# The end of a three-stage kernel: the last slot sums added on TensorE, the combine weights turned by VectorE, the output multiplied transposed in fp32 row tiles, and freed buffers handed to the experts' loads

## The chip, the cores and the metric

One core of one Trainium2 chip runs the kernel. The metric is the device time of one execution in microseconds (us); for the kernel before it is the median of three runs.

## What is computed

Three stages follow each other. A local and a pooled attention give 2304 tokens of 512 features; a gated product turns each token x into (x w_a) * (x w_b) w_out; a soft mixture of experts closes. Only the last stage is touched by the change:

```python
logits = x @ phi                      # 2304 tokens x 32 slots
d = softmax of logits over the tokens
slot_input = d.T @ x                  # 32 slots x 512, eight experts of four slots
h = np.maximum(slot_input[e] @ w1[e], 0.0)
slot_out[e] = h @ w2[e]               # w1, w2: 8 x 512 x 1024 and 8 x 1024 x 512, fp32
c = softmax of logits over the slots
return (c @ slot_out).astype(np.float32)
```

## The kernel before

The tokens are cut into six groups of 384 (`GS`, `NG = 6`). For every group twelve units of 128 hidden features run on TensorE (`plan_unit`: `half(0)`, `half(1)`, L1076), VectorE multiplies the two halves (`gmul`, L1091) into the group's buffer `g`, and after four units `logits` (L1099) multiplies them by `wpr`, the router folded with w_out, 32 columns at a time into four column groups of one PSUM bank.

`plan_chain(c)` is the softmax of a group. ScalarE copies the logits (`k1`), a matmul with `rep` adds the four column groups (`k2`, L1145), VectorE takes the maximum (`k3`, L1151, L1153), ScalarE forms the correction factor `al` and the exponentials (`k4`, L1159, L1163), VectorE turns the exponentials (`k6`, L1181) and the features (`turn`, L1107), TensorE sums the tokens of each slot in 32x32 tiles (`k11`, L1222, four PSUM banks), and VectorE adds them to the running sum `acc` (`k12`, L1235: acc = acc * al + new). The same chain makes the combine weights `cn` (`kl` to `k10`).

After the last group comes `plan_tail`. `atr` (L1325) multiplies `acc` by `rep32`, which adds its four parts and turns them; `slot_in` (L1351) applies w_out; `si_tr` (L1363) turns the slots; `l1` (L1392) runs the first expert layer, `htr` (L1408) turns its result, `l2` (L1480) runs the second layer in three pieces of 256, 128 and 128 output columns (`PARTS`). For each piece `so_sum` (L1500) gathers the slots' outputs, `so_hi` and `so_lo` (L1505, L1509) split them in two fp32r parts, `om` (L1527) multiplies by the combine weights, `oe` copies PSUM to SBUF (L321 on ScalarE, L323 on VectorE) and `od` (L1540) stores. The combine weights are turned by `ctr` (L1448, 18 transposes of 128x128 on TensorE) and split by L1451 and L1458 into `cT`. Where the planner expects TensorE to wait, `fill` (L370) issues matmuls that nobody reads.

The experts' weights come in 64 loads of 512 KB (L1297), in the order in which they are used; the first 32 are w1, the others w2. All loads and stores stand in one queue (SP). A load waits for a buffer of the list `e4`; buffers join it when the work that held them is done: weights of the gated product, `x` of the last group, `g` of the last two groups, the tiles `ot` of w_out after `slot_in`, and each expert buffer after its use.

A planner (`Plan.run`) puts all tasks in an order at build time by durations written beside them; on the chip the order on each engine is fixed, and the waits are semaphores.

Of the kernel before, what the change touches and what calls it, by code (L numbers as in the profile page):

```python
# [108 lines left out]
def tokens_of(o):  # L109

    o, parts = o.reshape(-1), []
    for c0, w in PARTS:
        t = o[c0 * NTILES * 128:(c0 + w) * NTILES * 128].reshape(128, NTILES, w)
        parts.append(t.transpose(1, 0, 2).reshape(NTILES * 128, w))
    return np.concatenate(parts, 1)
# [166 lines left out]
def tile_attn_glu_softmoe(  # L282
# [323 lines left out]
    def plan_datt(b):  # L606
        pr = PR_D[b] + 1

        def dvload2(j):
            if j == 0:  # L610
# [21 lines left out]
        def dvmm(f):  # L632

            if f:
                X.pop("vdt")
# [358 lines left out]
    def plan_rows():  # L994

        for n in range(12):
# [10 lines left out]
            def stage(n=n, fc=fc, m=m):  # L1007
                r0 = fc * 512 + m * 128
                nc.sync.dma_start(out=X["ost"][n % 2], in_=w_out[r0:r0 + 128, :])

            def low(e, n=n):
                clow(X["ost"][n % 2], e)

            def ab(n=n):
                X["op", n] = psum()
                cabs(X["ost"][n % 2], X["op", n])

            def bits(n=n):
                cbits(X["ost"][n % 2], X["op", n])

            def sign(n=n, fc=fc, m=m):
                csign(X["ost"][n % 2], X.pop(("op", n)), X["o", fc, m])
# [14 lines left out]
    def plan_wprime(fc):  # L1037
# [12 lines left out]
        def e3():  # L1050
            nc.scalar.copy(out=wpr[:, fc * 4:fc * 4 + 4, :], in_=X.pop(("wq", fc)))
# [4 lines left out]
        T["wpr", fc] = add("A", 0.3, e3, [t], -5, rel=("ps",))  # L1056
# [11 lines left out]
    def plan_unit(g, k, n):  # L1068
        fc, fi = divmod(k, 4)
        gt = GS[g]  # L1070

# [23 lines left out]
        def logits():  # L1095
            if fc == 0:
                X["lg", g] = psum((128, gt))
            for y in range(4):
                nc.tensor.matmul(  # L1099
                    out=X["lg", g][y * 32:y * 32 + 32, :], lhsT=wpr[:, fc * 4 + y, :], rhs=X["g", g][:, fc * 4 + y, :],  # L1100
                    start=(fc == 0), stop=(fc == 2),
                )

        def turn(y):

            t = X["g", g][:, fc * 4 + y:fc * 4 + y + 2, :].rearrange("p a b -> p (a b)")
# [14 lines left out]
        if fi == 3:  # L1121
            t = add(
                "PE", gt * 0.00167 + 0.1, logits, [T["gt", g, fc * 4 + y] for y in range(4)] + [T.get(("lgl", g))] + [T["wpr", f] for f in range(3)],
# [3 lines left out]
            for y in (0, 2):  # L1127
                T.setdefault(("g", g), []).append(add("V", gt / 480 + 0.17, lambda y=y: turn(y), [t], -15 + 0.1 * fc))

# [5 lines left out]
    def plan_chain(c):  # L1135
        gt = GS[c]
        nt, t0 = gt // 128, G0[c] // 128

# [4 lines left out]
        def k2():  # L1143
            X["lt", c] = ps = psum((128, gt))
            nc.tensor.matmul(  # L1145
                out=ps, lhsT=rep, rhs=X["lgs", c], start=True, stop=True
# [8 lines left out]

        def k4():
            if c > 0:
                X["al", c] = sb(mp, "al", (128, 1))
                nc.scalar.activation(  # L1159
                    out=X["al", c], in_=X.pop(("nm", c - 1)), func=ACTF.Exp, bias=X["nm", c], scale=-1.0  # L1160
                )
# [65 lines left out]
        def k12():  # L1227
# [11 lines left out]
        t2 = add("PE", gt * 0.00167 + 0.02, k2, [t1], p - 1000, acq=("ps",))  # L1239
        t3 = add("V", gt / 960 + 0.2, k3, [t2, T.get(("k3", c - 1))], -28, acq=("nm",))  # L1240
        T["k3", c] = t3
        t4 = add(
            "A", 0.9 if c else 0.6, k4, [t3], -28, acq=(("al",) if c else ()) + ("sm",), rel=("nm",) if c else (),
        )
        t5 = add("V", 0.15, k5, [t4, T.get(("k5", c - 1))], -20, acq=("L",), rel=("sm",) + (("L",) if c else ()))
        T["k5", c] = t5
        t6 = add("V", gt / 960 + 0.17, k6, [t4], -28, acq=())
        tl = add("V", 0.9, kl, [t3], -27, acq=("lc",))
# [6 lines left out]
        held = [add("N", 0.0, lambda: None, [t3], 0, acq=("ps",), lat=0.0) for _ in range(4)]  # L1255
        t11 = add("PE", gt * 0.007 + 0.1, k11, [t6] + T["g", c] + held, p - 1000, rel=("lgs", "g"), part="32x32")
        t12 = add(
            "V", 2.4, k12, [t11, t5, T.get(("k12", c - 1))], -18, rel=("ps",) * 4 + (("al",) if c else ())
        )
        T["k12", c], T["k2", c], T["k11", c] = t12, t2, t11  # L1260


    def plan_tail():
# [13 lines left out]
        g = NG - 1  # L1277
        give(T["mm", g], (), 3, lambda: (X.pop(("xh", g)), X.pop(("xl", g)), X.pop(("xt", g)), cut(sb(mp, "x", (128, 8 * GT)), 3))[3])
# [43 lines left out]
        def atr():  # L1322
            X["aps"] = ps = psum((128, 12, 32))
            for k in range(12):
                nc.tensor.matmul(out=ps[:, k, :], lhsT=acc[:, k].rearrange("p q j -> p (q j)"), rhs=rep32, start=True, stop=True)  # L1325

        def aev():
            t = sb(X["tp"], "tl", (128, 512))
# [10 lines left out]
        ta = [add("A", 0.5, aev, [t], -50, rel=("ps",))]  # L1339
# [46 lines left out]
        for eg in range(2):  # L1386
            for hf in range(2):
# [30 lines left out]
                for dt in range(4):  # L1418
                    w = tw[0, eg, hf, dt]
                    t = add(  # L1420
                        "PE", 0.94, lambda dt=dt, l1=l1: l1(dt), [t_si[dt // 2], t] + w, 3000 + eg * 2 + hf,
# [3 lines left out]
                t = add("PE", 0.5, htr, [t] + hs[-1:], -1000, acq=("ps",), rel=("ht",))  # L1425
# [3 lines left out]
        def ct():  # L1429
            X.pop(("xh", NG - 2)), X.pop(("xl", NG - 2)), X.pop(("xt", NG - 2))  # L1430
            t = sb(mp, "x", (128, NTILES, 128), F32R)
            for x in range(0, NTILES, 2):
                X["cT", x] = t[:, x:x + 2, :]

        t_ct = add("N", 0.0, ct, T["mm", NG - 2], 0, lat=0.0)
        tc_ = []
        n = 2
        for i0 in range(0, NTILES, n):

            def crep(e, i0=i0, n=n):  # L1440
                X["c4", i0] = t = sb(X["tp"], "ht", (128, n, 4, 32))
                copy(e, t, view(cn, [[32, n], [0, 4], [1, 32]], i0 * 32))

            def ctr(i0=i0, n=n):
                X["ctp", i0] = ps = psum((128, n, 128))
                t = X.pop(("c4", i0))
                for i in range(n):
                    nc.tensor.transpose(out=ps[:, i, :], in_=t[:, i, :, :], identity=ident)  # L1448

            def chi(i0=i0, n=n):  # L1450
                nc.scalar.copy(out=X["cT", i0], in_=X["ctp", i0])  # L1451

            def clo(i0=i0, n=n):
                ps = X.pop(("ctp", i0))
                cT = X["cT", i0]
                for r0 in (32, 96):
                    r = slice(r0, r0 + 32)
                    nc.vector.tensor_tensor(  # L1458
                        out=cT[r], in0=ps[r], in1=cT[r].bitcast(F32), op=ALU.subtract
                    )  # L1460

            t = add("V", 0.4, crep, [t_ct, T["open"]] + [T["cn", c] for c in sorted({GROUP[i0], GROUP[i0 + n - 1]})],
                    50, acq=("ht",), alt=("G", 0.5))
            t = add("PE", 0.12 * n, ctr, [t],
                    3000 + i0 * 0.01 - 10, acq=("ps", "ctp"), rel=("ht",))
            t = add("A", 0.2 * n, chi, [t], 50)

            tc_.append(add("V", 0.86, clo, [t, T["k12", NG - 1] if i0 < 8 else t_si[1]], 50, rel=("ps", "ctp")))

        for dh, (col0, w) in enumerate(PARTS):  # L1470
# [15 lines left out]
            for eg in range(2):  # L1486
                for m in range(8 // nf):
                    tl = tw[1, dh, eg, m]
                    prev = add(
                        "PE", 1.02, lambda eg=eg, m=m, l2=l2: l2(eg, m), [hs[eg * 2 + (m * nf + nf - 1) // 4], prev] + tl,  # L1490
# [11 lines left out]
            def so_hi(dh=dh, cols=cols):  # L1502
                if dh == 0:
                    X["s4"] = sb(X["tp"], "ht", (128, 512), F32R)
                nc.scalar.copy(out=X["s4"][:, cols], in_=X["sop", dh])  # L1505

            def so_lo(dh=dh, cols=cols):
                lo = X["s4"][64:128, cols]
                nc.vector.tensor_tensor(out=lo, in0=X.pop(("sop", dh))[64:128], in1=lo.bitcast(F32), op=ALU.subtract)  # L1509

            t = add("A", 0.15 + 0.22 * w / 256, so_ev, [prev], -40, acq=("a",), rel=("ps",))
            t = add("PE", 0.43 * w / 256, so_sum, [t], -1000, acq=("ps",), rel=("a",))
            t = add("A", 0.15 + 0.22 * w / 256, so_hi, [t, T.get("s4")], -40, acq=() if dh else ("ht",))
            T.setdefault("s4", t)
            t = add("V", 0.38, so_lo, [t], -40, rel=("ps",))
            pend = []

            ng = -(-NTILES // nf)
            for c in range(ng):
                i0, n = c * nf, min(nf, NTILES - c * nf)  # L1520

                def om(c=c, i0=i0, n=n, cols=cols, dh=dh, w=w):
                    if c % 2 == 0:
                        X["ob", dh, c // 2] = X["e4"].pop(0)
                    X["om", dh, c] = psum((128, n, w))
                    for x in range(n):
                        nc.tensor.matmul(  # L1527
                            out=X["om", dh, c][:, x, :], lhsT=X["cT", (i0 + x) // 2 * 2][:, (i0 + x) % 2, :],
# [120 lines left out]
```

## Time and profile before

| | |
|---|---|
| median of three runs | 518.35 us (517.28 to 519.37) |
| span of the profiled execution | 515.9 us |
| runs' median less that span | 2.45 us |
| TensorE matmuls busy | 493.5 us, 96% of the span |
| VectorE, ScalarE, GpSimd busy | 282.1, 194.7, 129.1 us |
| share of the chain that ended last on TensorE | 67% |
| HBM read, written | 78.81 MB, 4.72 MB |

The profiled execution shows no time of its own beside its span; the three runs were timed apart from it, so the difference of 2.45 us holds what lies around the span and the scatter between executions. Busy time of TensorE counts the filling matmuls too, so it doesn't say what work remains; the chain of work that ended last does, stretch by stretch. Times in the rows are counted from the start of the span.

### The profile page before, as it was taken

How to read it: one execution, taken by the hardware profiler on the slowest of the kernel's cores; microseconds unless marked ns; L12 is line 12 of the kernel's file. 1: busy time of each engine (PE TensorE's matmuls, PEld its weight loads, DVE VectorE, ACT ScalarE, POOL GpSimd, SP SyncE). 2: the span in 40 equal slices, each digit the busy share in tenths (PEclk: the TensorE clock that was granted, in tenths of full speed). 3: DMA queues.
4: the chain of work that ended last, by engine and by line, in shares of the span. 5: the costliest groups of instructions: out<-in, count | busy, mean ns of one | idle time of the engine just before them, and what ended most of it. 6: DMA issues, size and time to landing. Idle time of an engine off the chain costs nothing.

```text
span 515.9 us, 12483 instructions
## 1 busy us (share of the span) xinstructions
PE 493.5 (96%) x5182; PEld 427.6 (83%) x5182; DVE 282.1 (55%) x621; ACT 194.7 (38%) x469; POOL 129.1 (25%) x192
## 2 busy tenths in 40 slices
PE   8899999998999999999998999999999999999995
PEld 7788878977888788998887998879999997984474
DVE  5798888449934477213876322572553616365022
ACT  0986878645444232211342222232434212112132
POOL 1499886518720100100446000120000000000000
PEclk9999999999999999999999999999999999999998
DMA  8948772256752000000442000202678555998998
GB/s 314 352 134 252 259 236 90 83 164 204 234 194 82 1 1 3 1 1 22 157 160 52 1 1 0 62 4 84 209 279 271 170 180 166 336 338 289 410 408 335
DMA packets 30265, 84.35 MB, mean 163 GB/s; under 512 B 3456, under 2 KB 4480, under 8 KB 30208
## 3 DMA queue, kind: packets, MB, share of 16 engines
q1 hardware_dynamic: 30208, 83.54, 46.9%
q8 instruction: 41, 0.67, 0.5%
q14 instruction: 16, 0.13, 0.1%
HBM read 78.81 MB, written 4.72 MB: 162 GB/s over the span
## 4 chain that ended last, share of the span: by engine, by line
PE 67%; POOL 10%; DVE 9%; DMA 7%; ACT 3%; issue 3%; POOLq 0%; DVEq 0%; ACTq 0%
PE ps L1076 43%; DMA qk<-in_qk_dram 3%; PE ps L1480 3%; PE ps L1392 3%; POOL e L326 3%; PE ps L1099 3%; POOL w L326 3%; PE ps L1222 2%; POOL dT L448 2%; PE ps L366 2%; DMA bv<-in_vd_dram 2%; PE ps L542 1%; PE ps L1527 1%; DMA w<-in_moe_w_a_dram 1%; DMA sw<-in_w_outt_dram 1%
## 5 line engine op out<-in xcount | busy, mean ns | idle before, releaser
L1076 PE MATMUL ps<-x,w 128*128 128x384 f32 x1728 | 319.1, 339 | 0.9 <-DVE x L326 0.9
L1076 PEld LDWEIGHTS ps<-x,w 128*128 128x128 f32 x1728 | 297.5, 188 | 14.7 <-issue 8.9
L1091 DVE TENSOR_TENSOR g<-a,ps 128x384 f32<-128x384 f32 x72 | 39.5, 549 | 81.6 <-PE ps L1076 76.9
L321 ACT COPY a<-ps 128x384 f32<-128x384 f32 x72 | 34.5, 479 | 123.3 <-PE ps L1076 116.7
L1107 DVE STREAM_TRANSPOSE g<-g 128x768 f32<-128x768 f32 x36 | 32.6, 951 | 10.1 <-PE ps L1099 10.0
L1209 POOL TENSOR_TENSOR cn<-lc,cs 128x96 f32<-128x96 f32 x6 | 2.1, 349 | 118.9 <-DVE cs L1206 118.9
L326 POOL TENSOR_TENSOR w<-w,w 128x512 fp32r<-128x512 f32 x20 | 26.7, 1341 | 7.4 <-ACT w L321 7.2
L366 PE MATMUL ps<-acc 128*128 128x128 f32 x152 | 22.2, 301 | 2.2 <-POOL acc L361 2.2
L326 POOL TENSOR_TENSOR e<-e,mx 128x512 f32<-128x512 f32 x20 | 21.3, 1067 | 6.7 <-DVE mx L518 6.7
L366 PEld LDWEIGHTS ps<-acc 128*128 128x128 f32 x152 | 20.3, 212 | 2.8 <-POOL acc L361 2.2
L887 DVE SCALAR_TENSOR_TENSOR ps<-ps,w8x 128x512 uint32<-128x512 uint32 x12 | 8.4, 699 | 22.4 <-ACT ps L883 22.3
L551 DVE TENSOR_TENSOR xn<-ps,xd 128x232 f32<-128x232 f32 (+1 forms) x40 | 13.8, 388 | 12.3 <-PE ps L542 11.6
L446 POOL TENSOR_TENSOR dT<-qk 128x116 f32<-128x116 f32 (+1 forms) x18 | 8.8, 489 | 41.1 <-DMA qk<-in_qk_dram 41.1
L887 DVE SCALAR_TENSOR_TENSOR ps<-ps,sw 128x512 uint32<-128x512 uint32 x16 | 11.1, 695 | 14.0 <-ACT ps L883 14.0
L448 POOL TENSOR_TENSOR dT<-dT,qk 128x116 f32<-128x116 f32 (+1 forms) x36 | 18.0, 499 | 2.8
L528 PE MATMUL ps<-cst,e 128*128 128x128 f32 x80 | 12.7, 281 | 6.2 <-POOL e L326 6.2
L878 ACT ACTIVATE w8x<-w8x 128x512 uint32<-128x512 uint32 x12 | 8.1, 672 | 27.1 <-DMA w8x<-in_moe_w_out_dram 27.1
L326 POOL TENSOR_TENSOR x<-xn,x 128x464 fp32r<-128x464 f32 (+5 forms) x10 | 8.7, 877 | 38.1 <-ACT x L321 38.1
L542 PEld LDWEIGHTS ps<-e,bv 64*64 64x64 f32 x640 | 12.4, 133 | 6.8 <-ACT e L321 3.0
L326 POOL TENSOR_TENSOR dk<-de,dm 128x128 f32<-128x128 f32 x9 | 3.6, 402 | 55.7 <-DVE dm L708 55.5
L878 ACT ACTIVATE w<-w 128x512 uint32<-128x512 uint32 x20 | 13.5, 681 | 9.7 <-DMA w<-in_moe_w_a_dram 6.0
L321 ACT CAST x<-xn 128x464 fp32r<-128x464 f32 (+5 forms) x24 | 12.0, 511 | 13.5 <-DVE xn L551 13.5
(163 smaller groups left out, 674.1 us busy)
## 6 DMA issues: line engine op xcount, KB each, us to landing
w<-in_moe_w_dram SPq DMA_DIRECT2D x39, 512.0 KB, 8.5
qk<-in_qk_dram SPq DMA_DIRECT2D x17, 480.0 KB, 5.0
w8x<-in_moe_w_dram SPq DMA_DIRECT2D x14, 512.0 KB, 7.9
sw<-in_w_outt_dram SPq DMA_DIRECT2D x12, 512.0 KB, 4.3
w8x<-in_moe_w_out_dram SPq DMA_DIRECT2D x12, 512.0 KB, 4.8
w<-in_moe_w_a_dram SPq DMA_DIRECT2D x10, 512.0 KB, 5.0
bv<-in_vw_dram SPq DMA_DIRECT2D x20, 256.0 KB, 3.5
w<-in_moe_w_b_dram SPq DMA_DIRECT2D x10, 512.0 KB, 4.3
```

The source lines that it names most:

```text
L321: nc.scalar.copy(out=out, in_=in_)
L326: (nc.vector if e == "V" else nc.gpsimd).tensor_tensor(**a)
L366: nc.tensor.matmul(out=X["warm"][:, 0:128], lhsT=acc[:, 0], rhs=acc[:, 0], start=True, stop=True)
L448: nc.gpsimd.tensor_tensor(out=dst, in0=dst, in1=one[r], op=ALU.add)
L542: nc.tensor.matmul(out=pss[hl][o:o + 64, hq // 2, bi * w:bi * w + w], lhsT=v[r, bi, hq, :], rhs=pt[r, hq, bi * 64:bi * 64 + w], start=True ...
L878: nc.scalar.activation(out=d, in_=d, func=ACTF.Copy, scale=31 / 32 * 2.0 ** -29, bias=-0.26)
L887: nc.vector.scalar_tensor_tensor(out=d, in0=d, scalar=3, in1=words(raw)[1], op0=ALU.logical_shift_left, op1=ALU.bitwise_or)
L1076: nc.tensor.matmul(out=ps, lhsT=X["w", fc, ab, fi // 2, wi][:, fi % 2, hq, :], rhs=X[x, g][:, hq, :], start=(hq == 0 and m == 0), stop=(hq ...
L1091: nc.vector.tensor_tensor(out=X["g", g][:, k, :], in0=X.pop(("a", g, k)), in1=X.pop(("mm", g, k, 1)), op=ALU.mult)
L1099: nc.tensor.matmul(out=X["lg", g][y * 32:y * 32 + 32, :], lhsT=wpr[:, fc * 4 + y, :], rhs=X["g", g][:, fc * 4 + y, :], start=(fc == 0), st ...
L1107: nc.vector.transpose(out=t, in_=t)
L1392: nc.tensor.matmul(out=X["l1", eg, hf][e * 32:e * 32 + 32, :], lhsT=X["siT"][:, dt, :], rhs=X.pop((0, eg, hf, dt, e)), start=(dt == 0), st ...
```

## The change

Eight edits, all of them at the end of the program but for one small copy and one load that is issued earlier.

1. In the last group the logits of units 8 to 10 are multiplied before the last half unit; those of unit 11 are added straight into the bank of the summed logits by one more matmul (`kd`) whose weights are `phis`, unit 11's router columns written four times side by side (one ScalarE copy in `plan_wprime`).
2. `k4` is split; the factor `al` is a task of its own. In the last group the exponentials come ahead of the turning of the logits (`kl`).
3. The last group has no `k12`. `plan_sum` instead scales `rep32` by `al` (`scaled`), adds the old `acc` into a fresh PSUM bank (`old`, four matmuls of 32 columns), copies the four new sums into `acc` (`out`, two on ScalarE and two on VectorE) and adds them into the same bank (`new`, four matmuls).
4. `atr` is gone: VectorE turns that bank into `aT`.
5. The combine weights are turned in place by one VectorE instruction of 128x576 (`turned`); the copies, transposes and splits of `cT` are gone.
6. `so_hi`, `so_lo` become one fp32 copy. `om` now has the slots' outputs as weights and the combine weights as moving operand: four matmuls of 32 rows x 128 columns x 288 tokens, each in its own row group and PSUM bank; eight such sets instead of three times 18 matmuls. `oe` copies 32 pieces of 288 columns.
7. The output lies transposed in memory: twelve stores of 864, 864 and 576 columns; the host puts it in order again.
8. `e4` gets five buffers more: three of the fifth group's `x` (before: `cT`), one more `w8x`, and two thirds of `acc` after `new`.

```diff
             for y in range(4):
+                if last and fc * 4 + y == 11:
+                    break
                 nc.tensor.matmul(
                     out=X["lg", g][y * 32:y * 32 + 32, :], lhsT=wpr[:, fc * 4 + y, :], rhs=X["g", g][:, fc * 4 + y, :],
...
+        def kd():
+            nc.tensor.matmul(
+                out=X["lt", c], lhsT=phis.rearrange("p a b -> p (a b)"), rhs=X["g", c][:, 11, :], start=False, stop=True
             )
...
+    def plan_sum():
...
+        def scaled():
+            X["alr"] = phis[:, 0, :]
+            nc.vector.tensor_scalar_mul(out=X["alr"], in0=rep32, scalar1=X["al", c])
+
+        def old():
+            X["sum"] = ps = psum((128, 384))
+            t = X.pop("alr")
+            for q in range(4):
+                nc.tensor.matmul(out=ps[q * 32:q * 32 + 32, :], lhsT=t, rhs=acc[:, :, q, :], start=True, stop=False)
+
+        def out(q, e):
+            copy(e, acc[:, :, q, :], X["da", c][q].rearrange("p (k j) -> p k j", k=12))
+
+        def new(q):
+            nc.tensor.matmul(out=X["sum"][q * 32:q * 32 + 32, :], lhsT=rep32, rhs=acc[:, :, q, :], start=False, stop=True)
...
+        for g in (NG - 2, NG - 1):
+            give(T["mm", g], (), 3, lambda g=g: (
+                X.pop(("xh", g)), X.pop(("xl", g)), X.pop(("xt", g)), cut(sb(mp, "x", (128, 8 * GT)), 3))[3])
...
-            nc.scalar.copy(out=X["aT"], in_=X.pop("aps"))
-
-        t = add("PE", 1.35, atr, [T["k12", c9]], -2000, acq=("ps", "tl", "lgs", "a"))
+            nc.vector.transpose(out=X["aT"].rearrange("p a b -> p (a b)"), in_=X.pop("sum"))
...
+        def turned():
+            t = cn.rearrange("p m s -> p (m s)")
+            nc.vector.transpose(out=t, in_=t)
...
+                    def om(hh=hh, d0=d0):
+                        for q in range(4):
+                            r = slice(32 * q, 32 * q + 32)
+                            X["om", d0, hh * 4 + q] = ps = psum((128, 288))
+                            nc.tensor.matmul(
+                                out=ps, lhsT=X["s4"][r, d0:d0 + 128], rhs=cn[r, 9 * hh:9 * hh + 9, :].rearrange("p m s -> p (m s)"),
+                                start=True, stop=True,
+                            )
```

TensorE, from the end of the gated product to `slot_in`. Before (matmuls that write 32 rows use 32 columns of the array; `cst` holds `ident`, `rep` and `rep32`):

```order
L370 MATMUL ps<-cst 128x128 x3
L1099 MATMUL ps<-g,wpr 32x384 x4
L370 MATMUL ps<-cst 128x128 x4
L1145 MATMUL ps<-lgs,cst 128x384
L370 MATMUL ps<-cst 128x128 x14
L1222 MATMUL ps<-g,lgs 32x384 x48
L370 MATMUL ps<-cst 128x128 x12
L1325 MATMUL ps<-cst,acc 128x32 x12
L1448 MATMUL ps<-cst,ht 128x128 x4
L370 MATMUL ps<-cst 128x128
L1351 MATMUL ps<-w8x,a 32x256 x12
```

The same place in the changed kernel, from behind the last half unit (three logits matmuls, L1104, stand ahead of that half):

```order
L1156 MATMUL ps<-lgs,cst 128x384
L1161 MATMUL ps<-g,phis 128x384
L367 MATMUL ps<-cst 128x128 x8
L1298 MATMUL ps<-acc,phis 32x384 x4
L367 MATMUL ps<-cst 128x128
L1239 MATMUL ps<-g,lgs 32x384 x48
L367 MATMUL ps<-cst 128x128 x4
L1304 MATMUL ps<-acc,cst 32x384 x4
L367 MATMUL ps<-cst 128x128 x4
L1402 MATMUL ps<-w8x,a 32x256 x24
```

The logits matmul between the last unit and the sum is replaced by `kd` (L1161); the old sum (L1298) stands ahead of `k11` (L1239), the new one (L1304) behind it in the place of `atr`; both halves of `slot_in` (L1402) follow each other without a transpose between them.

TensorE, the last rows of the program. Before:

```order
L1480 MATMUL ps<-w_5009,tl 32x128 x8
L1480 MATMUL ps<-w_5037,tl 32x128 x8
L1500 MATMUL ps<-a,cst 128x128
L1527 MATMUL ps<-ht,x 128x128 x18
```

In the changed kernel:

```order
L1496 MATMUL ps<-w8x,acc 32x128 x8
L1535 MATMUL ps<-cn,ht 128x288 x4
L1496 MATMUL ps<-w8x,acc 32x128 x8
L1496 MATMUL ps<-w_4887,acc 32x128 x8
L1516 MATMUL ps<-a,cst 128x128
L1535 MATMUL ps<-cn,ht 128x288 x8
```

The product with the combine weights (L1535) comes in sets of four between the loads' matmuls of `l2` (L1496), six sets ahead of the last `so_sum` (L1516) and two behind it.

SP's queue around the end of the fifth group's units. Before:

```order
L1297 DMA w_5009<-in_moe_w_dram 128x1024
L1297 DMA w_5036<-in_moe_w_dram 128x1024
L1297 DMA w_5037<-in_moe_w_dram 128x1024
L1297 DMA w_5172<-in_moe_w_dram 128x1024
```

In the changed kernel:

```order
L1349 DMA w_5012<-in_moe_w_dram 128x1024
L1349 DMA x<-in_moe_w_dram 128x1024 x3
L1349 DMA w_5037<-in_moe_w_dram 128x1024
L1349 DMA w_5038<-in_moe_w_dram 128x1024
```

Three loads into the fifth group's `x` stand ahead of the next pair of weight buffers. One more load into `w8x` stands at the start of the experts' loads, so each later buffer takes a load that stands four places further on in the list.

## Rows read from the trace of the kernel before

**Rows 1.** The page: span, and granted TensorE clock in 40 slices.

```profile
span 515.9 us, 12483 instructions
...
PEclk9999999999999999999999999999999999999998
```

**Rows 2.** Chain that ended last, 440 to 470: start, us, what it waits in.

```profile
446.67 0.22 PE ps L1448 x2
446.89 2.12 PE ps L1076 x12
...
449.89 0.84 PE ps L1099 x8
450.73 1.82 DVE g L1107 x2
452.55 0.47 DVE nm L1151
...
453.04 0.16 DVE nm L1153
...
454.37 0.68 ACT lgs L1163 x2
...
455.07 0.59 DVE lgs L1181
...
455.70 2.77 PE ps L1222 x94
458.47 2.88 PE ps L370 x24
461.35 2.60 PE ps L1325 x24
...
464.64 1.43 PE ps L1351 x24
466.07 0.37 PE ps L1448 x2
...
469.18 1.85 PE ps L1392 x16
```

**Rows 3.** The same chain, 470 to its end.

```profile
480.23 3.57 PE ps L1392 x32
...
497.26 2.32 PE ps L1527 x18
...
503.76 2.16 PE ps L1527 x18
505.92 1.05 PE ps L1480 x32
...
508.64 2.02 PE ps L1527 x16
...
510.69 0.69 DVE w L323
```

**Rows 4.** Timeline, single instructions: start, us, engine, line, shapes, count.

```profile
449.11 0.56 DVE L1091 TENSOR_TENSOR g<-a,ps 128x384 f32<-128x384 f32 x1 [1.89 <-PE ps L1076]
...
451.60 0.81 PE L1145 MATMUL ps<-lgs,cst 128*128 128x384 f32 x2
...
458.46 2.19 DVE L1235 SCALAR_TENSOR_TENSOR acc<-acc,al,ps 128x384 f32<-128x384 f32 x4 [2.04 <-PE ps L1222]
...
463.98 0.48 ACT L1336 COPY a<-ps 128x384 f32<-128x384 f32 x1 [8.04 <-PE ps L1325]
```

**Rows 5.** Timeline of TensorE: four matmuls in two row tiles, early in the kernel.

```profile
81.01 0.77 PE L671 MATMUL ps<-dT,dT 64*128 64x144 f32 x8
```

**Rows 6.** Windows: stretch, busy time by engine, then granted clock, DMA share, GB/s.

```profile
420.00:440.00 20.00, 20.00 (x200) 16.91 (x199) 10.50 (x23) 4.28 (x14) 0.35 (x1) 1.00 0.52 170
460.00:470.00 10.00, 10.00 (x112) 7.46 (x114) 6.33 (x17) 2.62 (x7) 0.86 (x2) 1.00 0.74 247
500.00:510.00 10.00, 8.77 (x186) 7.72 (x175) 2.63 (x6) 3.67 (x9) 0.00 (x0) 1.00 1.03 412
```

More of the change, by code (lines that the diff above doesn't have):

```diff
@@ L109, in tokens_of @@
 def tokens_of(o):
[L111 to L115, printed above, removed]
+    o = o.reshape(512, 2, 4, NTILES // 2, 32).transpose(1, 3, 2, 4, 0)
+    return np.ascontiguousarray(o).reshape(NTILES * 128, 512)
 def rows_of(w):
@@ L1070, in plan_unit @@
         gt = GS[g]
+        last = g == NG - 1
         def half(ab):
@@ L1120, in plan_unit @@
         T["gt", g, k] = tg
-        if fi == 3:
+        if last and k == 11:
+            return
+        if fi == 3 or last and k == 10:
             t = add(
-                "PE", gt * 0.00167 + 0.1, logits, [T["gt", g, fc * 4 + y] for y in range(4)] + [T.get(("lgl", g))] + [T["wpr", f] for f in range(3)],
+                "PE", gt * 0.00167 + 0.1, logits, [T["gt", g, fc * 4 + y] for y in range(fi + 1)] + [T.get(("lgl", g))] + [T["wpr", f] for f in range(3)],
                 n - 1000, acq=("lg", "ps") if fc == 0 else (), part="128x32",
@@ L1145, in k2 @@
             nc.tensor.matmul(
-                out=ps, lhsT=rep, rhs=X["lgs", c], start=True, stop=True
+                out=ps, lhsT=rep, rhs=X["lgs", c], start=True, stop=not last
+            )
+        def kd():
+            nc.tensor.matmul(
+                out=X["lt", c], lhsT=phis.rearrange("p a b -> p (a b)"), rhs=X["g", c][:, 11, :], start=False, stop=True
             )
@@ L1254, in plan_chain @@
         T["cn", c] = t10
-        held = [add("N", 0.0, lambda: None, [t3], 0, acq=("ps",), lat=0.0) for _ in range(4)]
+        held = [add("N", 0.0, lambda: None, [t3], 0, acq=("ps",), lat=0.0) for _ in range(5 if last else 4)]
+        T["held"] = held[-1]
         t11 = add("PE", gt * 0.007 + 0.1, k11, [t6] + T["g", c] + held, p - 1000, rel=("lgs", "g"), part="32x32")
+        T["k2", c], T["k6", c], T["k11", c], T["al", c] = t2, t6, t11, ta
+        if last:
+            return
         t12 = add(
@@ L1259, in plan_chain @@
         )
-        T["k12", c], T["k2", c], T["k11", c] = t12, t2, t11
+        T["k12", c] = t12
+    def plan_sum():
+        c = NG - 1
+        def scaled():
[10 more added lines that the diff above has]
+            nc.tensor.matmul(out=X["sum"][q * 32:q * 32 + 32, :], lhsT=rep32, rhs=acc[:, :, q, :], start=False, stop=True)
+        t = add("V", 0.2, scaled, [T["al", c]], -28)
+        to = add("PE", 0.86, old, [t, T["k12", c - 1], T["held"]], -3000, part="128x32")
+        T["sum"] = []
+        for q in range(4):
+            e = "AV"[q % 2]
+            t = add(e, 0.5, lambda q=q, e=e: out(q, e), [T["k11", c], to], -60, rel=("ps",))
+            T["sum"].append(add("PE", 0.22, lambda q=q: new(q), [t], -2000 + q, part="128x32"))
     def plan_tail():
@@ L1320, in plan_tail @@
         t_sc = add("V", 0.3, scale, [T["k5", c9]], -20)
[L1322 to L1325, printed above, removed]
+        whole = acc.rearrange("p k q j -> p (k q j)")
+        rest = whole[:, 1024:1536]
+        give(T["sum"], (), 1, lambda: [whole[:, 0:1024]])
         def aev():
-            t = sb(X["tp"], "tl", (128, 512))
+            t = rest
             X["aT"] = sb(mp, "a", (128, 12, 32))
@@ L1424, in plan_tail @@
                 t = add("A", 0.58, relu, [t], -40, acq=("ht",), rel=("ps",))
-                t = add("PE", 0.5, htr, [t] + hs[-1:], -1000, acq=("ps",), rel=("ht",))
+                t = add("PE", 0.6, htr, [t] + hs[-1:], -1000, acq=("ps",), rel=("ht",))
                 hs.append(add("V", 0.25, hev, [t, t_z], -40, rel=("ps",)))
[L1429 to L1468, printed above, removed]
+        def turned():
+            t = cn.rearrange("p m s -> p (m s)")
+            nc.vector.transpose(out=t, in_=t)
+        t_cn = add("V", 0.77, turned, [T["cn", c] for c in range(NG)] + ta, 50)
         for dh, (col0, w) in enumerate(PARTS):
```

138 lines of the change are left out of this document (71 added, 67 removed).

## The prediction

> **What bounds the kernel now.** I read first the page's granted clock, then the chain of work that ended last, stretch by stretch, then the timeline for what one instruction costs, last the windows for the transfers. TensorE has its full clock (2.4 GHz) in every slice but the last [rows 1], so durations of before may be carried over. The chain in the last 75 us is TensorE nearly throughout, but what it does falls in two kinds. From 449.01 us (446.89 + 2.12), where the gated product ends, to 469.18, where the first expert layer starts, TensorE waits for a serial chain over VectorE and ScalarE; the 24 filling matmuls of 2.88 us behind `k11` and the three steps on VectorE and one on ScalarE between 450.73 and 455.66 are such waits [rows 2]. From 469.18 to 506.97 (505.92 + 1.05) the chain is TensorE's own work, and no transfer stands in it [rows 3]. So a shorter chain in the first stretch moves all of the second forward, as long as the weights are there. The reader should see in the windows that the DMA engines are full at 500 to 510 (412 GB/s), idle a quarter of 460 to 470 and half of 420 to 440 [rows 6].
>
> **The change part by part.** All sums are on the profiled execution, span 515.9 us.
>
> A. Gated product's end to `k11`. Before: 449.01 to 455.70, 6.69 us [rows 2]. After: two transpose pairs ahead of the end fall out (0.22 each, one shown), three logits matmuls come in; they run beside each other as the four do now, 0.84 [rows 2]. The end is then at 449.01 - 0.44 + 0.84 = 449.4. `k2` (0.81) runs while VectorE multiplies the last unit (0.56) [rows 4]; `kd` behind it is of the same size, so the logits' sum is there 1.6 later, at 451.0. The maximum takes from 452.55 to 453.20 now, 0.65 [rows 2]; take 0.7, so 451.7. The factor `al` is a small ScalarE instruction; I take 0.4 with its waits, under the 0.47 of the small steps here, since no row of the chain has it alone; then the exponentials 0.68 and their turning 0.59 [rows 2]: 453.4. Gone from the path are the turning of the features (1.82; three quarters now stand ahead of the last unit's product, the rest runs while ScalarE works) and the 1.17 from 453.20 to 454.37 in which ScalarE waited for VectorE's other turnings. `old` stands ahead of `k11` on TensorE and waits for `scaled`, which waits for `al` at about 452.1: 452.4 + 0.84 [rows 2] = 453.3, just in time; each tenth that `scaled` is late delays `k11` by the same. Gain 455.70 - 453.4 = **2.3**. Bounds: 1.5, if `old` is late by 0.8, its whole length; 2.8, if `kd` starts as soon as the product is there and the small step takes half.
>
> B. `k11`'s end to `slot_in`. Before: 458.47 to 464.64, 6.17 us [rows 2], of which 2.19 are `k12` [rows 4] and 2.60 `atr` [rows 2]. After: two copies on each engine; ScalarE 0.48 each, VectorE, by a quarter of `k12`, 0.55 each, so 1.1 [rows 4]. The last `new` matmul then takes what `k2` takes, 0.81 [rows 4]; the other three have gone ahead in other column groups. The turning of 384 columns is 0.59 [rows 2]. With 0.15 for waits: 2.65. Gain **3.5**. Bounds: 2.2, if the four `new` follow each other by half of 0.81 and the turning out of PSUM takes twice 0.59 less overlap; 3.7, without the waits.
>
> C. `slot_in` to the experts. Before: 464.64 to 469.18, 4.54 us [rows 2]. After: two halves of 1.43, 2.86 [rows 2]; then a copy of 256 columns (0.48 is the price of 384 [rows 4]; take 0.45), waits and two small matmuls, together 0.95. Gain 4.54 - 3.81 = **0.7**. Bounds: 0.37, the transpose pair alone [rows 2], to 1.0.
>
> D. The experts up to the last load's matmuls. Before: 469.18 to 506.97, 37.8 us. Out: two transpose pairs of 0.37, one of them shown [rows 2], and 36 matmuls of `om`, 2.32 + 2.16 [rows 3], together 5.2. In: six sets of four. The price of a set: 32 records of 512 columns, two per fp32 matmul, four column groups at a time, take 3.57 [rows 3]; that is 8 passes, 0.45 per 512 columns, so 0.25 per 288, and 0.50 for the two passes of a set if its four row groups run together. Leaving the experts' tiling and coming back costs 0.15: the same transpose pair takes 0.37 among the experts and 0.22 within the gated product [rows 2]. So 0.65 a set, 3.9. Gain **1.3**. No row has four row groups with 128 columns. Lower end 0.50; upper end, one group after the other, 8 x 0.25 + 0.15 = 2.15. Two rows speak for the lower: `k11`, four row groups by four column groups, makes 96 passes of 384 columns (0.33 each, 32 us in a row; 94 are recorded) in 2.77 [rows 2], and four matmuls in two row groups with 128 columns make 8 passes of 144 (0.125 each, 1.0 in a row) in 0.77 with start and end [rows 5]. I take 0.65, next to `k11`.
>
> The Trainium skill, TensorE: Matmul & The Clock Gate, Part 3 on the measured speedup, gives 3.07 times for four row tiles of 512 columns, not 4. The eight sets would each be 2.0 / 3.07 + 0.15 = 0.80, and the time 1.2 us later than mine, an estimate from that page, inside my range and with its chance in the forecast's; `k11` here shows more than 11 at a time out of 16 [rows 2].
>
> E. The end. Before: 506.97 to 515.9, 8.9 us: 1.67 to `om`, 2.02 of it, the last copy to 511.38 (510.69 + 0.69) [rows 3], and 4.5 of store and closing. After: the split on VectorE falls out, 0.3; the first copies can start after one set (0.65 + 0.1); eight copies of 288, five on ScalarE at some 0.35 (0.48 is 384 columns alone [rows 4]) make 1.75. So 1.35 + 0.75 + 1.75 = 3.85 instead of 4.4. The stores at the end are 0.44 and 0.29 MB instead of 0.52 and 0.13; I keep 4.5. Gain **0.6**; bounds 0 to 1.2.
>
> Costed at nothing: the turning of `cn` (576 of the 768 columns that take 0.91 [rows 2]) runs on VectorE under the 2.86 of `slot_in`; the first `om` needs it some 25 us later. Uncovered it would cost 0.7. Behind it in VectorE's queue stand the two small copies for the experts, needed 3.5 us later. The last group's `cn` comes later, under the same cover. The `phis` copy runs under the gated product.
>
> Sum: 2.3 + 3.5 + 0.7 + 1.3 + 0.6 = 8.4 us; the span becomes 507.5. Medians lie 2.45 above the span now; I leave that as it is: 518.35 - 8.4 = **509.9 us**.
>
> **Does the supply of weights follow?** A load of 0.524 MB takes 1.27 us at 412 GB/s [rows 6]. Four loads move into the stretch 420 to 440, where 48% of 20 us, 9.6, are free [rows 6]; that takes 5.1 out of the full stretch, and the earlier release of `g` and `ot` closes most of the 2.6 idle at 460 to 470 [rows 6]. Together 7.7 for 8.4 wanted, and no load stands in the chain now [rows 3], so there is room in hand. The three loads into `x` stand in SP's queue ahead of two weight buffers; a late `x` would hold those two as well.
>
> **Rivals.**
> 1. The weights set the end. If only one of the four loads falls in the free stretch, the full stretch shortens by 1.3 + 2.6 = 3.9: 514.5. For it: the DMA share is 1.03 at the end [rows 6]. Against it: the four need 5.1 us where 9.6 are free [rows 6]. 8 in 100.
> 2. Row groups one after the other, the case on the other side: a set takes 2.15, eight sets 12.0 more than mine: 518.35 - 8.4 + 12.0 = 522. It decides from 0.65 + 8.4 / 8 = 1.7 us a set on. Against it [rows 2, 5]. 6 in 100.
> 3. The clock falls. The filling matmuls from the product's end to `slot_in` go from 34 to 17, and TensorE waits in shorter pieces for copies. At the lower level (1.2 GHz) `k11`, `new`, `slot_in` and the small matmuls, 6.9 us, take twice as long: 516.9. Against it: in 500 to 510, with waits between 506.97 and 508.64, the granted clock was 1.00 [rows 6]. 5 in 100.
> 4. The first stretch isn't what it seems: another task of VectorE or ScalarE (the last group's combine weights, `kl` to `k9`) stands where `out` wants to run, and A and B give half, 2.9 less: 512.8. `kl` now comes after the exponentials, so these end near 456.3, when `k11` does. 10 in 100.
>
> **How the numbers follow.** The forecast has 71 in 100, its own range, from the bounds, 507.5 to 512.5. Less than 0.5% (2.6 us) can't be told from no change. Faster by more: forecast, rivals 1 and 4, 0.87 after some taken off for what I don't see; within: rival 3 and the like, 0.06; slower: rival 2 and the like, 0.07. The range for 8 in 10 takes in rival 4 and most of 1: 506.5 to 514.0.
>
> **What would show it.** In the changed profile: A, `k11` (L1239) starts 4.0 us after the last unit's matmul instead of 6.7, with `old` ended before; B, `slot_in` (L1402) starts 2.65 after `k11` ends; C, `l1` (L1443) 3.8 later; D, each set of L1535 adds about 0.65 to the chain; E, last copy 3.85 after the last `l2`. Wrong would be: a transfer in the chain behind L1443 or L1496 (rival 1), L1535 sets over 1 us (2), a granted clock under 1.00 at 445 to 465 (3), `out` waiting for VectorE's or ScalarE's own queue (4).

## The result and the profile after

The changed kernel takes 511.51 us (median of 4 runs, 510.29 to 514.01) beside 518.29 for the kernel before (4 runs); the ratio is 0.9867, 95% interval 0.9829 to 0.9906. By the ratio that is 6.9 us less (6.8 by the medians), where 8.4 were predicted; 509.9 stands against 511.5, and the range (506.5 to 514.0) holds the measured time.

The profiled run was the slowest of the four (span 512.2, time 514.01). The page says why its early part doesn't count:

```profile
span 512.2 us, 12347 instructions
...
PEclk9999999999999999999998999999999999999999
```

In one slice (the 22nd, 269 to 282 us), long ahead of the change, the granted clock was under full (0.87 on average), which it wasn't in [rows 1]. That holds back what comes behind it, by 1.7 us at most (0.13 of 12.8); the rest of the 2.7 us by which the mark below is late is scatter of the early part, for in the other runs of this document the mark lies anywhere between 435.9 and 439.4. I therefore read both traces from this mark, a point that the change doesn't touch: the end of the fifth group's `k11`, where the next product starts. Before:

```profile
437.90 4.36 PE ps L1076 x24
```

In the changed kernel it is at 440.56, and from there the chain of waits runs as follows (start, us, what), to be held against [rows 2, 3]. The count behind an x is of records, two for each fp32 matmul:

```profile
440.56 8.55 PE ps L1079 x48
449.11 0.78 PE ps L1104 x6
449.89 2.32 PE ps L1079 x12
...
452.31 0.57 DVE g L1094
...
452.92 0.91 PE ps L1161 x2
453.83 1.78 PE ps L367 x16
455.61 0.78 PE ps L1298 x8
456.40 0.42 PE ps L367 x2
456.81 2.70 PE ps L1239 x94
459.51 1.09 PE ps L367 x8
460.60 0.85 PE ps L1304 x8
461.45 1.09 PE ps L367 x8
462.54 2.73 PE ps L1402 x48
...
466.52 5.29 PE ps L1443 x48
...
491.69 1.01 PE ps L1496 x32
492.71 0.70 PE ps L1535 x8
...
502.36 1.05 PE ps L1496 x32
...
504.77 1.38 PE ps L1535 x16
...
506.86 0.30 ACT w L318
```

The reader should see four things: `k11` (L1239) begins 4.6 us after the product's end at 452.21 instead of 6.7; `k12` and `atr` are gone, and between `k11` and `slot_in` (L1402) stands `new` (L1304) alone, among filling matmuls (L367); the two blocks of `om` between the `l2` matmuls in [rows 3] have become six sets of 0.70, and the one behind them two sets at the end; nothing in it is a transfer. The windows say the same of the clock, and something else of the transfers (busy times, then granted clock, DMA share, GB/s):

```profile
420.00:440.00 20.00, 20.00 (x198) 17.41 (x202) 8.74 (x19) 4.28 (x14) 0.35 (x1) 1.00 0.60 201
440.00:460.00 20.00, 19.93 (x226) 15.52 (x198) 9.61 (x25) 3.82 (x14) 0.35 (x1) 1.00 0.98 343
460.00:470.00 10.00, 10.00 (x116) 5.43 (x118) 2.25 (x6) 1.30 (x3) 0.53 (x1) 1.00 1.01 354
...
490.00:500.00 10.00, 10.00 (x236) 6.80 (x229) 2.56 (x6) 4.92 (x14) 0.00 (x0) 1.00 0.96 374
500.00:510.00 10.00, 5.12 (x98) 3.16 (x98) 2.46 (x6) 3.95 (x12) 0.00 (x0) 0.99 0.78 300
```

Against [rows 6] the idle quarter of 460 to 470 is closed, and the slack has moved to the end, 0.78 instead of 1.03.

Cut into five stages at the chain's own marks, every run below can be compared without its early part. The stages are: fifth group's `k11` end to the last `k11`; that `k11`'s end to `slot_in`; `slot_in` to `l1`; `l1` to the end of the last `l2`; from there to the end of the span (known to a tenth, and with it the last stage and the sum).

```
                   to k11  to slot_in  to l1  to last l2   end    sum
before              17.80     6.17      4.54    37.79      8.93  75.23
after               16.25     3.03      3.98    36.89      8.79  68.94
after, again        16.25     3.03      3.98    36.89      8.79  68.94
no fills            15.66     2.71      4.05    36.90      8.82  68.14
no early loads      16.24     3.03      3.98    36.89     12.20  72.34
old sum             16.14     6.45      4.04    36.89      8.85  72.37
old chain           17.14     6.45      4.04    36.90      8.78  73.31
one edit back (kd)  17.22     3.02      3.98    36.90      8.87  69.99
old output          18.07     3.69      4.48    38.29      8.89  73.42
one row group       16.25     3.02      3.99    45.50     11.69  80.45
pairs               15.64     2.71      4.05    36.89      8.59  67.88
pairs, again        15.66     2.71      4.05    36.89      8.54  67.85
```

The sum falls by 6.29 us from before to after; with `k11` itself (2.77 in [rows 2], 2.70 now) that is 6.4, beside 6.9 by the ratio.

### The profile page after: what moved, and what is told of

Same layout as the page of the kernel before. It is cut to its first block, busy times and chain, and to the rows that moved or that the text cites. A ratio compares the mean times of both kernels' runs of the same rounds, so it can differ in the third digit from the quotient of the medians.

```text
span 512.2 us, 12347 instructions
## 1 busy us (share of the span) xinstructions
PE 489.0 (95%) x5134; PEld 418.5 (82%) x5134; DVE 272.5 (53%) x600; ACT 193.9 (38%) x471; POOL 127.8 (25%) x189
## 4 chain that ended last, share of the span: by engine, by line
PE 67%; POOL 9%; DMA 8%; DVE 8%; ACT 3%; issue 3%; POOLq 0%; ACTq 0%; DVEq 0%
PE ps L1079 44%; DMA qk<-in_qk_dram 3%; PE ps L1496 3%; PE ps L1443 3%; PE ps L1104 3%; POOL w L323 2%; POOL e L323 2%; PE ps L1239 2%; DMA w<-in_moe_w_a_dram 2%; PE ps L363 2%; POOL dT L445 2%; DMA bv<-in_vd_dram 2%; PE ps L539 1%; PE ps L1535 1%; DMA sw<-in_w_outt_dram 1%
## 5 line engine op out<-in xcount | busy, mean ns | idle before, releaser
L1112 DVE STREAM_TRANSPOSE g<-g 128x768 f32<-128x768 f32 (+1 forms) x37 | 32.7, 930 | 11.3 <-PE ps L1104 11.2
L525 PE MATMUL ps<-cst,e 128*128 128x128 f32 x80 | 12.8, 283 | 7.2 <-POOL e L323 7.2
L525 PEld LDWEIGHTS ps<-cst,e 128*128 128x128 f32 x80 | 8.9, 142 | 11.0 <-POOL e L323 10.4
```

The lines of the kernel that those rows point to most:

```text
L525: nc.tensor.transpose(out=ps[:, hq, :], in_=e[:, hq, :], identity=ident)
L1112: nc.vector.transpose(out=t, in_=t)
```

## The experiments

Each of the eight kernels undoes or alters one part of the change. Ratios are to the kernel before, which ran on the same chip.

**No filling matmuls.** The function that issues them does nothing.

```
-        for _ in range(n):
-            nc.tensor.matmul(out=X["fill"], lhsT=ident, rhs=ident, start=True, stop=True)
+        return
```

> The changed kernel, but its 34 filling matmuls of 1.78, 0.42, 1.09 and 1.09 us between the gated product's end and slot_in (and one of 0.30 in front of l1) are not issued. Theory: the chain has no wait left that they are needed for, and they hold TensorE past the moment at which old and slot_in could start (old stands behind a fill of 1.78 us, slot_in behind one of 1.09 us whose input was there about 0.35 us earlier). Then k11 comes about 0.5 us and slot_in about 0.35 us earlier, the clock stays at 1.00, and the time is 0.5 to 1.0 us under the changed kernel's, 510.5 to 511. Rival (rival 3 of the prediction, the clock): without them the granted clock of 455 to 470 falls to about half, k11, new, slot_in and the small matmuls take up to twice as long, and the time is up to 6.9 us more, near 518.

Measured: 510.34 us, ratio 0.9828 (0.9792 to 0.9864), 2 us under the changed kernel by the difference of the ratios, whose intervals overlap. Its chain in the same stretch, and its window of 450 to 460:

```profile
447.59 0.03 issue
...
449.99 0.49 DVE g L1111
450.48 0.13 DVE phis L1291
...
450.75 0.85 PE ps L1297 x8
451.60 2.72 PE ps L1238 x94
454.32 0.47 ACT acc L318
...
454.83 1.54 PE ps L1303 x8
...
457.03 2.87 PE ps L1401 x48
```

```profile
450.00:460.00 10.00, 8.05 (x162) 3.85 (x163) 5.40 (x17) 3.29 (x13) 0.87 (x2) 1.00 0.99 368
```

The fills that are left out are 17 matmuls in front of `slot_in`, 34 records, and one in front of `l1`. `k11` follows the product's end (447.59) by 4.01 us, where 4.0 was predicted, and `slot_in` follows `k11`'s end by 2.71, where 2.65 was. TensorE was busy for 8.05 us of 10 and its granted clock stayed at 1.00. So the rival is refuted for these waits, and the fills cost 0.8 us in the stages (0.6 in front of `k11`, 0.3 in front of `slot_in`, less 0.1 later). The row of `phis` (`scaled`) is where `old` waits now, behind a turning of 0.49 on VectorE; the turned exponentials, which `k11` needs too, are there at 451.49, so a faster `old` would gain no more than 0.1.

**No early loads.** The last edit undone: four loads go back behind buffers that come free later, and the buffer of `acc` isn't given.

```
-        for g in (NG - 2, NG - 1):
+        for g in (NG - 1,):
...
-        give(T["sum"], (), 1, lambda: [whole[:, 0:1024]])
...
-    cs=3, w8x=11, e4=0,
+    cs=3, w8x=10, e4=0,
```

> The changed kernel without its last edit: only the last group's x buffer is given to the experts' loads and the accumulator's 4 KB buffer isn't given, so four loads of 0.524 MB go back behind buffers that come free later, while all of the shorter chain stays. Rival 1 in its strong form (the supply of weights is what the time hangs on, and the shorter chain only moves the wait): TensorE waits for loads among the experts, and nearly all of the gain goes, 516 to 518. Theory: the chain and the supply had about 2 us in hand before; four loads of 1.27 us later are 5.1 us, of which the 6 us of shorter chain leave some 2 to 3 uncovered at the last load: 513 to 514.5. Third case: no load is missed at all, within 0.5 us of the changed kernel; then the last edit brings nothing.

Measured: 515.39 us, ratio 0.9938 (0.9907 to 0.9970): 3.7 us of the 6.9 are lost, by the difference of the ratios. The size is between theory and rival; the place is in neither. The stages up to the last `l2` are those of the changed kernel to a hundredth, so no matmul waits for a weight; the whole loss is in the end, 12.20 us instead of 8.79. Chain, windows and DMA issues (count, KB each, median us from issue to landing):

```profile
505.24 0.30 ACT x L318
```

```profile
505.00:507.00 2.00, 0.00 (x0) 0.00 (x0) 0.25 (x1) 0.55 (x2) 0.00 (x0) 1.00 1.02 409
507.00:509.00 2.00, 0.00 (x0) 0.00 (x0) 0.00 (x0) 0.00 (x0) 0.00 (x0) 0.54 1.03 414
```

```profile
out_dram<-w SPq DMA_DIRECT2D x6, 432.0 KB, 7.2
out_dram<-g SPq DMA_DIRECT2D x2, 432.0 KB, 7.9
out_dram<-w SPq DMA_DIRECT2D x2, 288.0 KB, 8.0
```

The last copy is done at 505.54, 3.74 behind the last `l2` as in the changed kernel (3.75), and then the DMA engines still work at their full rate for more than 3 us: the stores stand behind the loads and land 7 to 8 us after their issue. In the changed kernel the same rows read:

```profile
out_dram<-w SPq DMA_DIRECT2D x6, 432.0 KB, 3.7
out_dram<-w SPq DMA_DIRECT2D x3, 288.0 KB, 3.9
```

So the supply does set the time here, but through the output, where a chain of waits on TensorE doesn't show it. The size is near what the windows give: behind the common mark 27.5 MB move instead of 25.4, four loads more; four loads of 1.27 us [rows 6] are 5.1 us; the changed kernel leaves 0.04 of 490 to 500 and 0.22 of 500 to 510 free, 2.6; so at least 2.5 must come out at the end. 3.4 did in the stages; that the difference is the free time behind the last copy, which loads can't use, is my reading.

**The old chain with the early loads.** Edits 1, 3 and 4 undone: `kd`, `scaled`, `old` and `new` out, `k12` and `atr` back. This is nearly the other corner, supply without chain; edits 2 and 5 to 7 stay.

```
-                out=ps, lhsT=rep, rhs=X["lgs", c], start=True, stop=not last
+                out=ps, lhsT=rep, rhs=X["lgs", c], start=True, stop=True
...
-            nc.vector.transpose(out=X["aT"].rearrange("p a b -> p (a b)"), in_=X.pop("sum"))
+            nc.scalar.copy(out=X["aT"], in_=X.pop("aps"))
...
-    plan_sum()
```

> The changed kernel with the first three edits of its chain undone (the last unit's logits go through the logits sum again, the slot sums are added on VectorE and turned by matmuls); its output part and its early loads stay, the accumulator's buffer being given after its turning. It has the early loads without the shorter chain, where the run without early loads had the shorter chain without the loads. Theory, after that run: chain and transfers are two paths of about one length in the kernel before, so that each alone brings less than its part; here the chain loses A and B again (1.6 + 3.1 us) and keeps C, D and E: 511.3 + 4.7 = 516, all stores landing within 4 us of the last copy. Rival: early loads bring a gain of their own, additive to the chain's; then this kernel keeps the 3.7 us that the run without early loads lost, and comes to 518.2 - 3.7 = 514.5 or less.

Measured: 516.51 us, ratio 0.9953 (0.9931 to 0.9975), 2.4 us under before, and 1.9 by the stages: the gains of C, D and E and 0.7 of the first stage, less 0.3 in the second. The rival's 514.5 (0.993) lies just under the interval, and the stages leave nothing over that the loads would have brought by themselves. By the ratios the short chain without the early loads brings 3.2 us, the early loads with C, D and E 2.4, and all together 6.9. A kernel with the early loads and no other edit wasn't tried.

**The old sum.** Only edits 3 and 4 undone, in the way of the last two pieces of the diff above.

> The changed kernel with the last slot sums added on VectorE again and turned by matmuls (k12 and atr as before, the accumulator's buffer given after atr instead of after the sum on TensorE). Theory: only the stretch from k11's end to slot_in goes back, from 3.03 us to about 6.2, and the time rises by 3 us (2.2 to 3.7), to about 514.5. Rival (the experts wait for weights anyway, or the clock sets the stretch): no more than 1 us, under 512.5.

Measured: 514.29 us, ratio 0.9921 (0.9886 to 0.9956). That is 2.8 us above the changed kernel, as expected; the second stage is 6.45 us again, and 3.4 of the stages' 6.3 go back (the chain here shows 24 records of filling ahead of `atr`, as in [rows 2]):

```profile
455.07 2.88 PE ps L367 x24
457.95 2.60 PE ps L1378 x24
...
461.52 2.73 PE ps L1406 x48
```

**One edit back (`kd`).** Only edit 1 undone.

> The changed kernel with only the first edit undone: the logits of the last unit are added in the logits sum again, and all four turnings of the features stand ahead of k11 (the slot sums stay on TensorE). Theory: only the stretch from the gated product's end to k11 goes back, from 4.7 to about 6.3 us, the stretch from k11's end to slot_in stays 3.0, and the time rises by 1.3 to 1.6 us, to about 513. Rival 4 of the prediction (VectorE's and ScalarE's other tasks set this stretch in either form): under 0.5 us, and k11 as far behind the product's end as in the changed kernel.

Measured: 513.54 us, ratio 0.9883 (0.9846 to 0.9920). The first stage goes from 16.25 to 17.22: 0.97 us, less than expected; with the last unit's logits out of the sum, three logits matmuls (0.78) stand ahead of the product's end and still take TensorE's time, so the distance from the product's end to `k11`, 6.62 us against 4.60, overstates the edit. About 0.2 of the 0.97 is filling again: `k11` starts 0.91 behind the turned exponentials, in the changed kernel 0.69. Rival 4 is refuted all the same: the edit still shortens the stretch by more than the rival's 0.5, and in the changed kernel VectorE is idle ahead of its first `out` and waits for `k11`:

```profile
459.54 1.02 DVE L320 COPY acc<-ps 128x384 f32<-128x384 f32 x2 [0.50 <-PE ps L1239]
```

**One row group.** All four matmuls of a set read the first 32 rows.

```
-    out=ps, lhsT=X["s4"][r, d0:d0 + 128], rhs=cn[r, 9 * hh:9 * hh + 9, :]
+    out=ps, lhsT=X["s4"][0:32, d0:d0 + 128], rhs=cn[0:32, 9 * hh:9 * hh + 9, :]
```

> The changed kernel, but the four output matmuls of a set all read the first 32 rows of their two inputs, so that all four go to the same row group of TensorE; the output then holds the first quarter of the sum over rows four times over, and its time is that of as many matmuls of the same shape. Theory: in the changed kernel the four row groups run beside each other (0.70 us a set); in one row group they follow each other, 8 passes of 288 columns at some 0.125 to 0.25 us, so a set takes 1.0 to 2.15 us, by the prediction's upper bound 2.15, and the span is up to 10 to 12 us longer (eight sets by 1.45). Rival: the set is bound by something else (weights, PSUM) and takes 0.70 here too; then the row groups bring nothing.

Measured: 524.26 us, one run. Six sets in the chain now take, each:

```profile
491.49 2.13 PE ps L1535 x8
493.63 1.01 PE ps L1496 x32
```

2.13 us against 0.70, 8.6 us more in the fourth stage for six sets (1.43 each), and the rest in the end. The prediction's upper bound, 2.15, is what one group costs, and rival 2 would have been worked out rightly; it just isn't what four groups take here.

**The old output.** Edits 5 to 7 undone: combine weights turned on TensorE (with two PSUM buffers instead of three, since the sum needs one), 36 output matmuls, the x buffer of the last but one group not given.

> The changed kernel with the output as before: the combine weights turned on TensorE, the output multiplied with hi and lo halves of 36 matmuls, and so without the x buffer of the last but one group for the experts' loads (it holds the turned weights); the shorter chain stays. Theory: TensorE's stretch from l1 to the end of the last load's matmuls goes back from 36.9 to 37.8 us and the end from 8.8 to 8.9, and three loads come later, which by the run without early loads (3.7 us for four) costs 2 to 3 us more, seen as stores that land 5 us or more after their issue: 514 to 515.5. Rival: only the 1 us of the output itself, 512.3, with the stores landing as in the changed kernel.

Measured: 515.82 us, ratio 0.9942 (0.9919 to 0.9965), 3.9 above the changed kernel. The size is a little over the theory's, the reason is another: the last stores land 2.8 to 3.1 us after their issue, and the end is 8.89. What is longer are all stages of the chain. VectorE's own rows show one place (start, us, what, idle before):

```profile
459.48 1.02 DVE L323 COPY acc<-ps 128x384 f32<-128x384 f32 x2 [2.09 <-PE ps L1242]
460.53 1.74 DVE L1512 TENSOR_TENSOR x<-ps,x 32x256 fp32r<-32x256 f32 x4
462.30 0.58 DVE L1391 STREAM_TRANSPOSE a<-ps 128x384 f32<-128x384 f32 x1
```

The subtractions of the turned weights (L1512) run between the copies and the turning of the sum, which has nothing else to wait for once `new` has ended, at 461.39, and starts at 462.30. And `k11` comes 1.8 us later than in the changed kernel, with `old` at 455.97, though its input was there at 453.58. All the time between, TensorE runs filling matmuls, and the turned exponentials, the other input of `k11`, are long there:

```profile
452.18 3.79 PE ps L370 x34
```

```profile
453.89 0.58 DVE L1201 STREAM_TRANSPOSE lgs<-lgs 128x384 f32<-128x384 f32 x1 [0.31 <-ACT lgs L1183]
```

`k11` starts 2.29 us after that turning, in the changed kernel 0.69, so 1.6 of the 1.82 are filling; why the planner puts so much of it there wasn't tried (this version has two PSUM buffers for the turning). The first three stages lose 3.0 us (1.82, 0.66 and 0.50). Without the 1.6, 1.4 are left for the turning of the weights, where the prediction's sum had 0.44 in A and 0.37 in C for it. The old output costs 1.5 in the last two stages.

**Pairs.** No fills, and the last 128 columns go out in four stores of two copies.

```
+                np_ = 2 if d0 == 384 else 3
...
-                        if n % 3 == 2 or n == 7:
+                        if n % np_ == np_ - 1 or n == 7:
```

> The run without filling matmuls, and the last 128 output columns go out in four stores of two copies each instead of three of three, three and two. Theory: the end is set by the first of the last stores (2.45 us from issue to landing, then the rest at the rate of the DMA engines); with two copies to wait for it is issued 0.3 to 0.4 us earlier, and the end comes 0.3 us earlier, 8.5 us after the last load's matmuls instead of 8.8; the time is about 509, the best of all. Rival: SyncE takes 0.43 us for each issue, the fourth store leaves 0.1 to 0.4 us later than the third did, and the end stays or comes up to 0.4 us later.

Measured: 510.91 us, ratio 0.9840 (0.9804 to 0.9875); the end is 8.59 instead of 8.82, a gain of 0.2; by the ratio it can't be told from the kernel without fills (0.9828). Repeated beside the changed kernel on one chip:

> The changed kernel once more, unaltered, beside the best version on one chip. Expected: the ratio to the kernel before stays at 0.987 (0.983 to 0.991), and the stages of its profile from the fifth group's k11 to the end (16.2, 3.0, 4.0, 36.9 and 8.8 us) repeat within 0.1 us, whatever the time of the work ahead of them does.

> The version without filling matmuls and with stores of two copies at the end once more, beside the changed kernel on one chip. Theory: the stages are 15.6, 2.7, 4.0, 36.9 and 8.6 us, 1.1 us less than the changed kernel's, and the medians differ by that, 0.2%. Rival: the profile's gain isn't in the time (the clock of later stages, or a wait for the stores, takes it back): the medians agree within 0.3 us.

Measured: the changed kernel 512.28 us, ratio 0.9867 (0.9841 to 0.9894), its stages the same to a hundredth; pairs 510.38, ratio 0.9847 (0.9822 to 0.9872). The stages differ by 1.09 us as expected, the ratios by 0.2%, 1.0 us, the medians by 1.9; the intervals overlap, so by the time alone the better version is likely and not certain. By the stages it is the best here, about 8 us under before by its ratio.

## Why the prediction was right, and where its sizes were off

**A**, 2.3 predicted. Right in mechanism; measured 1.55 (17.80 to 16.25, of which 0.97 are `kd`). What was missing: eight filling matmuls of 1.78 us in a row stood ahead of `old`, and one of 0.42 behind it. The exponentials were turned at 456.12, `old` ended at 456.39, and `k11` started at 456.81:

```profile
455.54 0.58 DVE L1198 STREAM_TRANSPOSE lgs<-lgs 128x384 f32<-128x384 f32 x1 [0.31 <-ACT lgs L1180]
```

Without the fills the step comes out at 4.01 us, the prediction's 4.0. The other 0.15 are the product's end, 0.54 later than before from the mark where the prediction had 0.40. The lower bound of 1.5 had a late `old` in it, but not that the filling would be what holds it.

**B**, 3.5 predicted, 3.14 measured; 3.03 after instead of 2.65. Again filling: four matmuls of 1.09 us end behind the turning of the sum. Without them 2.71. The prediction also took all of the 2.88 us of filling ahead of `atr` for a wait [rows 2], and "24 filling matmuls" are 24 records, 12 matmuls. `k12` had ended at 460.65 [rows 4], 0.7 before `atr` began, and in the run with the old sum it is the same (457.25 and 457.95). So about 0.65 of the 3.14 is the filling of the kernel before, and not the way of adding; the kernel before without its fills wasn't tried.

**C**, 0.7 predicted, 0.56 measured, within its bounds.

**D**, 1.3 predicted, 0.90 measured. A set costs 0.70, not 0.65; over six sets that is 0.3. The rest is a balance that the sum left out: `l2`'s matmuls, cut in pieces by the sets, take 0.4 more (1.01 for 32 records, where 64 took 1.89), and those of `l1` 0.26 less (14.28 instead of 14.54). The Trainium skill, TensorE: Matmul & The Clock Gate, in Part 3's section on measured speedup, has four row tiles of 512 columns at 3.07 times; the runs here, with 288 columns, agree with it when a whole set is taken (2.13 / 0.70 = 3.04), whereas the prediction had divided only the matmuls' part and added 0.15. On the whole set, an estimate from the page's figure would have been 2.15 / 3.07 = 0.70.

**E**, 0.6 predicted, 0.14 measured: the step that was sized worst. The last copy ends 3.75 us after the last `l2` as predicted (3.85), but the stores' last 4.5 us became 5.0. The prediction counted them from the last copy. By the traces the last three stores, 1.18 MB in both kernels, take 4.4 us from the first one's issue to the last one's landing, before (510.6 to 515.0) as after (506.6 to 511.0). So what seems to count is when the first of them goes, and not the last copy. It goes 3.15 us after the last `l2` instead of 3.58, a gain of 0.43, and some 0.3 of it is lost again between the last landing and the end (about 1.2 instead of 0.9), for which no run shows a cause. The version with pairs, whose first issue comes after 2.87, gained 0.2.

**The supply**, predicted as able to follow (7.7 us for 8.4 wanted, and "room in hand"), did follow: no transfer stands in the chain of the changed kernel, and in the 12 us ahead of the common mark the DMA share is 0.81 instead of 0.48, so three of the four loads did move into the free stretch. Rival 1 didn't come true as it was put. But the room was smaller than "no load stands in the chain" let it seem. Without the early loads half of the gain is gone, and it goes at the stores, a place that rival 1's test ("a transfer in the chain behind L1443 or L1496") wouldn't have shown. The DMA share of 1.03 in 500 to 510 [rows 6] said it: chain and transfers ended together.

**Rival 3**, the clock: refuted twice, by 1.00 in all windows of 440 to 500 of the changed kernel, and by 1.00 in the run without any fill. **Rival 2** by 0.70 against 2.13, **rival 4** by the run with `kd` undone.

Between the predicted 8.4 and the stages' 6.3 lie 2.1 us: A 0.75 and B 0.36, of which the fills are 0.9, C 0.14, D 0.40, E 0.46. All five fall on one side, so the sum didn't come near by errors that cancel. The ratio gives 0.6 more gain than the stages, within the interval. The 2.45 us between median and span that the prediction carried over are partly scatter: a run's time lies 1.8 above its own span (514.01 and 512.2), so about 0.6 of the 2.45 was the profiled execution being a quick one. No step failed; the sizes of A, B, D and E were the ones that were off.

## What to carry to other kernels

When the chain of waits is compute to its end and the DMA share is over 1 in the same stretch, take it that there may be two bounds of about one length, as there were here, so that shortening one brings only part of its gain: bring loads forward in the same change, and look for the loss at the stores. Work that fills waits is itself a wait as soon as the waits get short; after a chain has been shortened, run it once without the filling, and the kernel before too, or part of the difference is that of the fills. The price of matmuls that share the array is best taken from two runs of one shape, in one row group and in four, since that gives the whole ratio with its switching.

## What was not expected of the hardware

Without any filling, TensorE's granted clock held 1.00 from 440 to 460 us, with 8.05 us of work in the second half and with single waits of up to 1.6 us. In the kernel with one row group it did fall: TensorE waited 0.55 and 0.35 us around L1516 (510.8 to 512.2), as it does in the changed kernel, and while it worked on the last two sets, one row group at a time, the clock went to 1.2 GHz:

```profile
512.00:514.00 2.00, 1.84 (x7) 1.45 (x8) 0.00 (x0) 0.91 (x3) 0.00 (x0) 0.96 0.05 16
514.00:516.00 2.00, 2.00 (x5) 1.33 (x4) 0.82 (x2) 0.23 (x1) 0.00 (x0) 0.50 0.00 0
```

```profile
512.16 6.47 PE ps L1535 x16
```

The two sets took 6.47 us there, 2.2 more than twice 2.13 and 5.1 more than the 1.38 of the changed kernel. The end is only 2.9 us longer, because the last copy ends 0.4 us behind the sets instead of 1.0 and the stores behind it take 3.45 us instead of 5.0. What made the clock fall with TensorE busy for 1.84 and 2.00 us of 2 wasn't tried.
